# Linear attention and two MLPs on one core: one ring of five PSUM banks for attention, decoding exponents two pieces ahead, first loads released in turn

## The chip, the cores and the metric

The kernel runs on 1 core of one Trainium2 chip. The core has TensorE (PE, matmuls), VectorE (DVE), ScalarE (ACT), GpSimd (POOL), SyncE (SP, which here only issues transfers), an SBUF of 128 partitions and a PSUM of 8 banks of 512 floats per partition. The metric is device time in microseconds; before the change it is 1017.65 us, the median of 3 runs (1014.94 to 1017.94).

## The reference

Three stages follow each other; all in float32:

```python
# attention, batch 4, 8 heads, 576 tokens, head_dim 64, 128 features
proj = x @ omega.T;  h = proj - |x|^2/2;  h = h - max(h);  phi = exp(h) / sqrt(128)   # for q and for k
kv  = sum_s phi_k[s] v[s];  z = sum_s phi_k[s]
att = (phi_q @ kv) / (phi_q @ z + 1e-6)
# MLP 1: 2304 tokens, 512 -> 2048 -> 512
h = x @ w_in;  g = max(h, 0) + alpha * min(h, 0);  x = g @ w_out
# MLP 2: 512 -> 1536 -> 512
x = ((x @ w_a) * (x @ w_b)) @ w_out
```

The weights come to the kernel as 64-bit words and are made into floats by the kernel itself, as below.

## The kernel before, in words

The order of the instructions on each engine is written out by hand; the framework adds the waits. Tiles come from pools with a number of buffers; a new tile waits until an old one of its pool has had its last reader, and a pool opened in the place of a closed one waits for the closed one.

**Attention** goes in steps `s` (line 649 on). A unit `u` is a batch and four heads (8 units), and each has 5 token tiles `t`. One step makes the projections of a k tile and, from step 6 (`Q_LAG`), of a q tile into a pair of PSUM banks (`a_proj`, L523), takes their maxima on DVE (`a_max`, L532), the exponentials on ACT (`a_exp`, L546, one instruction per head, first all of the first bank, then all of the second), then adds the k tile of the step before to the `kv` sum (L559, one bank; at the end of a unit ACT copies it, L565), takes numerator and denominator of an older q tile (`a_num`: bank `nd`, normalised on DVE, L597 to L600, into `xn`), transposes the last exponentials (`a_t`: bank `tp`, copied by ACT or DVE, L577/L579, to `phT`), and transposes an older result into `xT` (`a_x`, bank `xp`, L612 to L620). So from step 10 on a step takes five banks of the tag `ps`.

**The weights** are 68 pieces of 128x512 words. A piece `p` (class `Decoder`) is loaded as `raw` (512 KB, L115, SP). ACT makes the exponent `z` from its high words (L127) and in way 0 scales the low words (L132): that is `start(p)`. `piece(p)` is a generator that is advanced one turn at a time from the other work (`go`): shift of z (DVE, L145), a (L147), c (L150, in ways 1 and 2 also L153), then the high part `wh` on ACT (L158) and the low part `wl` by two or three operations on POOL, or on DVE in way 2 (L157, L159, L160). A fifth turn starts the exponent of piece p+1, if `ahead` is set. `raw` has 2 buffers. `z` has one PSUM bank (`psz`) in steps 0 to 13, and two SBUF buffers after. The pieces go into `NS` slots of SBUF, of which 20 exist during attention; a piece whose slot still holds a weight in use waits (`can`). A credit (`step`) sets how many pieces a step may begin: none in steps 0 to 2, half a piece in steps 3 to 5, then one per step; in the later MLP stages 0.35 to 0.5 per 384 columns. The way of a piece is picked by planned loads of DVE, ACT and POOL.

**Stage 1** is steps 0 to 13 (`SPLIT_AT` = 14): attention and decoding of pieces 0 to 8 alone. The banks are: kv 1, `psz` 1, `ps` 6. The transfers of k, v, q and raw are issued in `attn_1`, before the maxima, with those of units 0 and 1 and raw 0 and 1 at once. **Stage 2** opens `ps` anew with 5 banks, and `psy` with 2 banks for MLP 1's output sums: five chunks of 256 tokens of MLP 1's first half run (`Mlp.run`), and within each front (`a_front`: 12 matmuls into a bank of `ps`, L265) one more attention step is interleaved (`attn_next`); its order is projections, MLP's `high` (ACT), maxima, `low` (DVE), exponentials, rest. The inputs of the MLP are split into a high and a low part (`split`: `xh` on ACT L251, `xl` on DVE or POOL L254). **Then** attention's memory is given back, the remaining slots are opened, and the rest of MLP 1 and MLP 2 run in chunks of 512 and 256 tokens, with fronts (L265) and backs (L331, L386) alternating on PE.

Of the kernel before, what the change touches and what calls it, by code (L numbers as in the profile page):

```python
# [9 lines left out]
F32 = mybir.dt.float32  # L10
F32R = mybir.dt.float32r
U32 = mybir.dt.uint32
# [3 lines left out]
PSUM = bass.MemoryType.PSUM  # L16
# [23 lines left out]
CHUNKS = (512, 512, 256, 512, 512)  # L40
NS = 29
NS1 = 20
# [10 lines left out]
def tile_kernel(ctx: ExitStack, tc: tile.TileContext, qT, kT, v1, omT, wbits, alpha, out):  # L53
# [44 lines left out]
    class Decoder:  # L98
# [12 lines left out]

        def load(self, p):
            if p < NP and p not in self.raw:
                raw = dec.tile([P, DM, 2], U32, tag="raw", name=f"raw{p}")
                nc.sync.dma_start(out=raw.rearrange("p n t -> p (n t)"), in_=wbits[p].bitcast(U32))  # L115
                self.raw[p] = raw

        def start(self, p):
# [6 lines left out]
            pool = self.bank or dec  # L125
            z = pool.tile([P, DM], U32, tag="z", name=f"z{p}", bufs=1 if self.bank else 2)
            nc.scalar.activation(z.bitcast(F32), H.bitcast(F32), AF.Copy, scale=2.0 ** -112)  # L127
# [7 lines left out]
        def piece(self, p):  # L135
            self.start(p)
            self.load(p + 1)
            z, way = self.z[p]
            raw = self.raw[p]
# [21 lines left out]
            self.ready = p + 1  # L161
            yield
            if self.ahead and self.can(p + 1):
                self.start(p + 1)

# [317 lines left out]

    t_k, t_q, t_v = {}, {}, {}
    phik, phiq, phT, kvt, xns = {}, {}, {}, {}, {}
    psp = [None]

    def load_k(u):
        t = ld.tile([P, 2 * S], F32, tag="k", name=f"k{u}")
        if u == 0:  # L490
            nc.scalar.dma_start(out=t[:, 0:256], in_=kT[u][:, 0:256])
            nc.sync.dma_start(out=t[:, 256:], in_=kT[u][:, 256:])
        else:
            nc.sync.dma_start(out=t, in_=kT[u])
        t_k[u] = t

    def load_v(u):
        t = ld.tile([P, TT * VC], F32, tag="v", name=f"v{u}")
        nc.sync.dma_start(out=t, in_=v1[u])
        t_v[u] = t  # L500

    def load_q(u):
        t = ld.tile([P, 2 * S], F32, tag="q", name=f"q{u}")
        nc.sync.dma_start(out=t, in_=qT[u])
        t_q[u] = t
# [132 lines left out]
    def attn_1(s):  # L638
# [3 lines left out]
        else:  # L642
            pair = None
        if s in ev["k"]:
            u, t = ev["k"][s]
            if t == 0 and u + 1 < U:
                load_k(u + 1)
            if t == 2 and u + 1 < U:
                load_v(u + 1)
            if u == 0 and t > 2:  # L650
                load_q(t - 3)
        if s in ev["q"]:
            u, t = ev["q"][s]
            if t == 4 and u + 2 < U:
                load_q(u + 2)
        return pair and (pair, jobs)

    def attn_2(s):

        D_.go(2)  # L660
        if s in ev["kv"]:
# [4 lines left out]
        if s in ev["t"]:  # L666
            a_t(*ev["t"][s])
        D_.go(2)

# [14 lines left out]

    st_p = ExitStack()
    st_m = ExitStack()
    A = Mlp(st_m, CI, 2)
    st_z = ExitStack()
    D_.bank = rpool(st_z, name="psz", bufs=1, space=PSUM)
    with ExitStack() as st:  # L690
        psp[0] = rpool(st, name="ps0", bufs=6, space=PSUM)
        w_ = bank("warm")
        for i in range(WARM):
            nc.tensor.matmul(w_[:, 0:P], lhsT=warm, rhs=warm, start=True, stop=True)
        for s in range(SPLIT_AT):
            D_.step(DEC0[0] if s < 3 else DEC0[1] if s < Q_LAG else DEC0[2])
            passed(1.3 if s < Q_LAG else 4.5)
            D_.ahead = s < SPLIT_AT - 1
            pj = attn_1(s)
            if pj:  # L700
                a_exp(*pj, a_max(*pj))
            if s == Q_LAG:
                nc.sync.dma_start(out=nalpha, in_=alpha)
# [12 lines left out]
    with st_m:  # L716
        psp[0] = rpool(st_p, name="ps1", bufs=5, space=PSUM)
        A.banks((psp[0], "ps"))
# [3 lines left out]
        def attn_next(high=None, low=None):  # L722
# [6 lines left out]
            if pj:  # L729
                nm = a_max(*pj)  # L730
            if low:
                low()
# [37 lines left out]
        while nxt_s[0] < steps:  # L770
            attn_more()
        st_p.close()
    st_a.close()
# [78 lines left out]
```

## Time and profile before

| | |
|---|---|
| median of 3 runs | 1017.65 us (1014.94 to 1017.94) |
| profiled execution | 1018.62 us, span 1016.8 us, mean granted clock 0.985 |
| PE busy | 983.3 us (97% of the span), 6414 matmuls |
| DVE, ACT, POOL busy | 481.8, 440.5, 270.1 us |
| PE on the chain that ended last | ab L265 29%, o L386 14%, h L265 14%, y L331 14% of the span |

A time in the trace counts from the start of the span; the execution's own time is 1.8 us longer. Busy time says how long an engine had an instruction running. A wait is idle time of an engine put down to what ended it. PEclk is the share of the full clock that TensorE was granted.

### The profile page before, as it was taken

The page shows a single profiled execution, that of the slowest core. Times are in us where ns is not written, and L with a number is a line of the kernel's source. Part 1 is how long each engine was busy: PE and PEld are TensorE (multiplying, and loading weights), DVE is VectorE, ACT ScalarE, POOL GpSimd, SP SyncE. Part 2 cuts the span into 40 slices and gives each one's busy share as a digit, 9 for nine tenths or more (in the row PEclk, how much of TensorE's full clock was granted, in tenths as well). Part 3 has the DMA queues.
Part 4 walks back from the last instruction along what each step waited for, and adds up shares of the span by engine and source line. Part 5 has one row for each costly group of instructions (what it writes and reads, how often), then busy time and mean ns, then how long its engine had stood idle before and what let it go on. Part 6 is the DMA issues. An engine that isn't in the chain of part 4 may idle for free.

```text
span 1016.8 us, 15843 instructions
## 1 busy us (share of the span) xinstructions
PE 983.3 (97%) x6414; PEld 840.3 (83%) x6414; DVE 481.8 (47%) x934; ACT 440.5 (43%) x1027; POOL 270.1 (27%) x208
## 2 busy tenths in 40 slices
PE   7869899999999999999999999999999999999998
PEld 6658799999988888889888888898888888898886
DVE  4868855654456666445465434344133322132132
ACT  5878766654455555445445332232232321122110
POOL 2856510000024543434233332332223220000100
PEclk7879999999999999999999999999999999999999
DMA  7543523000012332312212112121020302011021
GB/s 268 193 152 111 163 86 96 25 23 2 32 52 87 100 119 90 104 42 63 83 45 80 42 42 83 42 84 62 21 83 22 124 1 83 1 63 63 1 83 41
DMA packets 27449, 75.16 MB, mean 74 GB/s; under 512 B 2288, under 2 KB 5616, under 8 KB 27376
## 3 DMA queue, kind: packets, MB, share of 16 engines
q1 hardware_dynamic: 27232, 74.02, 22.1%
q8 instruction: 50, 0.82, 0.3%
q14 instruction: 23, 0.19, 0.1%
q10 hardware_dynamic: 144, 0.13, 0.0%
HBM read 59.99 MB, written 14.16 MB: 73 GB/s over the span
## 4 chain that ended last, share of the span: by engine, by line
PE 71%; DVE 0%; POOL 0%; issue 0%; ACT 0%; POOLq 0%; ACTq 0%
PE ab L265 29%; PE o L386 14%; PE h L265 14%; PE y L331 14%; DVE opl L396 0%; POOL xl L254 0%; POOL wl L160 0%; DVE xl L254 0%; DVE a L147 0%; ACT wh L158 0%; DVE h L291 0%; POOL a L159 0%; ACT gh L302 0%; ACT u L289 0%; ACT h L290 0%
## 5 line engine op out<-in xcount | busy, mean ns | idle before, releaser
L159 POOL TENSOR_TENSOR a<-a,wh 128x512 f32<-128x512 f32 x68 | 100.9, 1483 | 315.6 <-ACT wh L158 310.9
L265 PE MATMUL ab<-xh,wh 128*128 128x512 f32 (+1 forms) x480 | 177.3, 369 | 0.0
L265 PE MATMUL ab<-xh,wl 128*128 128x512 f32 (+1 forms) x480 | 177.2, 369 | 0.0
L265 PE MATMUL ab<-xl,wh 128*128 128x512 f32 (+1 forms) x480 | 177.1, 369 | 0.0
L265 PE MATMUL h<-xh,wh 128*128 128x512 f32 (+1 forms) x384 | 133.5, 348 | 1.0 <-ACT xh L251 1.0
L265 PE MATMUL h<-xl,wh 128*128 128x512 f32 (+1 forms) x384 | 130.5, 340 | 1.4 <-POOL xl L254 1.2
L331 PE MATMUL y<-gh,wh 128*128 128x512 f32 (+1 forms) x384 | 131.3, 342 | 0.0
L265 PE MATMUL h<-xh,wl 128*128 128x512 f32 (+1 forms) x384 | 130.3, 339 | 0.0
L331 PE MATMUL y<-gh,wl 128*128 128x512 f32 (+1 forms) x384 | 129.4, 337 | 0.0
L331 PE MATMUL y<-gl,wh 128*128 128x512 f32 (+1 forms) x384 | 129.3, 337 | 0.0
L291 DVE SCALAR_TENSOR_TENSOR h<-u,nalpha,h 128x256 f32<-128x256 f32 (+1 forms) x96 | 59.6, 621 | 119.5 <-ACT h L290 116.5
L254 POOL TENSOR_TENSOR xl<-xT,xh 128x512 fp32r<-128x512 f32 (+1 forms) x33 | 38.3, 1162 | 272.0 <-ACT xh L251 267.8
L371 DVE TENSOR_TENSOR ab<-a,ab 128x512 f32<-128x512 f32 (+1 forms) x60 | 38.4, 641 | 143.4 <-PE ab L265 140.5
L265 PEld LDWEIGHTS ab<-xl,wh 128*128 128x128 f32 x480 | 90.4, 188 | 16.2
L265 PEld LDWEIGHTS ab<-xh,wh 128*128 128x128 f32 x480 | 90.4, 188 | 16.0
L265 PEld LDWEIGHTS ab<-xh,wl 128*128 128x128 f32 x480 | 90.4, 188 | 15.8
L160 POOL TENSOR_TENSOR wl<-a,c 128x512 fp32r<-128x512 f32 x68 | 89.8, 1321 | 5.3
L272 ACT ACTIVATE gh<-ab 128x512 fp32r<-128x512 f32 (+1 forms) x60 | 33.4, 556 | 123.0 <-DVE ab L371 123.0
L386 PE MATMUL o<-wh,gh 128*128 128x512 f32 x216 | 84.5, 391 | 0.0
L386 PE MATMUL o<-wh,gl 128*128 128x512 f32 x216 | 84.5, 391 | 0.0
L386 PE MATMUL o<-wl,gh 128*128 128x512 f32 x216 | 84.4, 391 | 0.0
L265 PEld LDWEIGHTS h<-xl,wh 128*128 128x128 f32 x384 | 73.6, 192 | 10.2 <-POOL xl L254 1.6
(314 smaller groups left out, 1658.7 us busy)
## 6 DMA issues: line engine op xcount, KB each, us to landing
raw<-in_w SPq DMA_DIRECT2D x68, 512.0 KB, 3.7
v<-in_v SPq DMA_DIRECT2D x8, 650.0 KB, 5.4
q<-in_qT SPq DMA_DIRECT2D x8, 576.0 KB, 3.8
out<-opl SPq DMA_DIRECT2D x18, 256.0 KB, 2.1
yp<-ypart SPq DMA_DIRECT2D x4, 1024.0 KB, 7.1
opart<-op SPq DMA_DIRECT2D x4, 1024.0 KB, 5.0
opl<-opart SPq DMA_DIRECT2D x4, 1024.0 KB, 5.6
k<-in_kT SPq DMA_DIRECT2D x7, 576.0 KB, 4.7
```

Of the source, the lines that this page charges most:

```text
L159: eng.tensor_tensor(out=a, in0=a, in1=hi.bitcast(F32), op=ALU.subtract)
L160: eng.tensor_tensor(out=lo, in0=a, in1=c, op=ALU.add)
L254: (nc.vector, nc.gpsimd)[way].tensor_tensor(out=lo, in0=src, in1=hi.bitcast(F32), op=ALU.subtract)
L265: nc.tensor.matmul(hp, lhsT=w_[:, ks], rhs=r_, start=(i == 0), stop=(i == 3 * KT - 1))
L272: nc.scalar.activation(gh, g, AF.Copy)
L291: nc.vector.scalar_tensor_tensor(out=hp, in0=u_, scalar=nalpha[:, f:f + 1], in1=hp, op0=ALU.mult, op1=ALU.add)
L331: nc.tensor.matmul(ys[e], lhsT=w_[:, es], rhs=r_, start=(first and i == 0 and head), stop=(last and i == 2 and tail))
L371: nc.vector.tensor_tensor(out=pp[1], in0=a_, in1=pp[1], op=ALU.mult)
L386: nc.tensor.matmul(os_[t], lhsT=w_[:, ts_], rhs=r_, start=(i6 == 0 and i == 0), stop=(i6 == 5 and i == 2))
```

## The change

- Attention has one pool `ps` of five banks for both stages, opened once. `psz` has two banks and lies where `psy` is opened later.
- A piece has four turns instead of five; at the end of the fourth it starts the exponent of piece p+2, not p+1, and loads raw(p+2) as well when it begins. `raw` has 3 buffers, `NS` is 28 instead of 29. The exponents of pieces 0 and 1 are started in steps 3 and 4. In steps 11 to 13 no exponent is started ahead (before: in step 13 alone). Starting ahead no longer asks whether the slot is free.
- In attention, three turns are taken before kv and numerator and one before the transposes; before it was two, one and two after the transposes.
- The transfers are issued in a function of their own, `loads`, after the maxima. In steps 0 to 3 those of k1, raw0 and q0, v1, raw1 and q1 each wait for a one-column memset on DVE into the tile, which stands behind the step's maxima. The load of alpha moves from step 6 to step 7.

```diff
--- before.py
+++ after.py
@@ -38,7 +38,7 @@
 CB = 512
 REST = (512, 512)
 CHUNKS = (512, 512, 256, 512, 512)
-NS = 29
+NS = 28
 NS1 = 20
 
 DEC0 = (0.0, 0.5, 1.0)
@@ -109,9 +109,11 @@
             self.z = {}
             self.ahead = True
 
-        def load(self, p):
+        def load(self, p, after=False):
             if p < NP and p not in self.raw:
-                raw = dec.tile([P, DM, 2], U32, tag="raw", name=f"raw{p}")
+                raw = dec.tile([P, DM, 2], U32, tag="raw", name=f"raw{p}", bufs=3)
+                if after:
+                    after_dve(raw[:, :, 0].bitcast(F32))
                 nc.sync.dma_start(out=raw.rearrange("p n t -> p (n t)"), in_=wbits[p].bitcast(U32))
                 self.raw[p] = raw
 
@@ -123,7 +125,7 @@
             raw = self.raw[p]
             L, H = raw[:, :, 0], raw[:, :, 1]
             pool = self.bank or dec
-            z = pool.tile([P, DM], U32, tag="z", name=f"z{p}", bufs=1 if self.bank else 2)
+            z = pool.tile([P, DM], U32, tag="z", name=f"z{p}", bufs=2)
             nc.scalar.activation(z.bitcast(F32), H.bitcast(F32), AF.Copy, scale=2.0 ** -112)
             way = pick({"dve": 1.9, "act": 2.0, "pool": 3.9}, {"dve": 2.6, "act": 1.35, "pool": 2.6},
                        {"dve": 3.9, "act": 1.35})
@@ -135,6 +137,7 @@
         def piece(self, p):
             self.start(p)
             self.load(p + 1)
+            self.load(p + 2)
             z, way = self.z[p]
             raw = self.raw[p]
             L, H = raw[:, :, 0], raw[:, :, 1]
@@ -159,9 +162,8 @@
             eng.tensor_tensor(out=a, in0=a, in1=hi.bitcast(F32), op=ALU.subtract)
             eng.tensor_tensor(out=lo, in0=a, in1=c, op=ALU.add)
             self.ready = p + 1
-            yield
-            if self.ahead and self.can(p + 1):
-                self.start(p + 1)
+            if self.ahead:
+                self.start(p + 2)
 
         def can(self, p):
             return p < NP and p % NS < len(slots) and (p < NS or self.free.get(p - NS, False))
@@ -482,6 +484,11 @@
     kvp = [ac.tile([P, 4, D + 1], F32, name=f"kvp{i}") for i in range(3)]
 
     t_k, t_q, t_v = {}, {}, {}
+
+    def after_dve(t):
+
+        nc.vector.memset(t[:, 0:1], 0.0)
+
     phik, phiq, phT, kvt, xns = {}, {}, {}, {}, {}
     psp = [None]
 
@@ -491,16 +498,22 @@
             nc.scalar.dma_start(out=t[:, 0:256], in_=kT[u][:, 0:256])
             nc.sync.dma_start(out=t[:, 256:], in_=kT[u][:, 256:])
         else:
+            if u == 1:
+                after_dve(t)
             nc.sync.dma_start(out=t, in_=kT[u])
         t_k[u] = t
 
     def load_v(u):
         t = ld.tile([P, TT * VC], F32, tag="v", name=f"v{u}")
+        if u == 1:
+            after_dve(t)
         nc.sync.dma_start(out=t, in_=v1[u])
         t_v[u] = t
 
     def load_q(u):
         t = ld.tile([P, 2 * S], F32, tag="q", name=f"q{u}")
+        if u < 2:
+            after_dve(t)
         nc.sync.dma_start(out=t, in_=qT[u])
         t_q[u] = t
 
@@ -641,23 +654,35 @@
             pair, jobs = a_proj(ev["k"].get(s), ev["q"].get(s))
         else:
             pair = None
-        if s in ev["k"]:
+        return pair and (pair, jobs)
+
+    def loads(s):
+        if s < TT:
+
+            if s == 0:
+                load_k(1)
+            elif s == 1:
+                D_.load(0, True)
+                load_q(0)
+            elif s == 2:
+                load_v(1)
+            elif s == 3:
+                D_.load(1, True)
+                load_q(1)
+        elif s in ev["k"]:
             u, t = ev["k"][s]
             if t == 0 and u + 1 < U:
                 load_k(u + 1)
             if t == 2 and u + 1 < U:
                 load_v(u + 1)
-            if u == 0 and t > 2:
-                load_q(t - 3)
         if s in ev["q"]:
             u, t = ev["q"][s]
             if t == 4 and u + 2 < U:
                 load_q(u + 2)
-        return pair and (pair, jobs)
 
     def attn_2(s):
 
-        D_.go(2)
+        D_.go(3)
         if s in ev["kv"]:
             a_kv(*ev["kv"][s])
         if s in ev["num"]:
@@ -665,7 +690,6 @@
         D_.go()
         if s in ev["t"]:
             a_t(*ev["t"][s])
-        D_.go(2)
 
     def attn_3(s):
         if s in ev["x"]:
@@ -682,24 +706,26 @@
     nc.vector.tensor_scalar(out=om, in0=om_raw, scalar1=scale, scalar2=None, op0=ALU.mult)
     load_v(0)
 
-    st_p = ExitStack()
     st_m = ExitStack()
     A = Mlp(st_m, CI, 2)
     st_z = ExitStack()
-    D_.bank = rpool(st_z, name="psz", bufs=1, space=PSUM)
-    with ExitStack() as st:
-        psp[0] = rpool(st, name="ps0", bufs=6, space=PSUM)
+    psp[0] = rpool(st_a, name="ps", bufs=5, space=PSUM)
+    D_.bank = st_z.enter_context(tc.tile_pool(name="psz", bufs=2, space=PSUM))
+    if True:
         w_ = bank("warm")
         for i in range(WARM):
             nc.tensor.matmul(w_[:, 0:P], lhsT=warm, rhs=warm, start=True, stop=True)
         for s in range(SPLIT_AT):
             D_.step(DEC0[0] if s < 3 else DEC0[1] if s < Q_LAG else DEC0[2])
             passed(1.3 if s < Q_LAG else 4.5)
-            D_.ahead = s < SPLIT_AT - 1
+            D_.ahead = s < SPLIT_AT - 3
             pj = attn_1(s)
-            if pj:
-                a_exp(*pj, a_max(*pj))
-            if s == Q_LAG:
+            nm = a_max(*pj)
+            loads(s)
+            a_exp(*pj, nm)
+            if s in (3, 4):
+                D_.start(s - 3)
+            if s == Q_LAG + 1:
                 nc.sync.dma_start(out=nalpha, in_=alpha)
             attn_2(s)
             attn_3(s)
@@ -714,7 +740,6 @@
     D_.ahead = True
 
     with st_m:
-        psp[0] = rpool(st_p, name="ps1", bufs=5, space=PSUM)
         A.banks((psp[0], "ps"))
         nxt_s = [SPLIT_AT]
         due = [0.0]
@@ -728,6 +753,7 @@
                 high()
             if pj:
                 nm = a_max(*pj)
+            loads(s)
             if low:
                 low()
             if pj:
@@ -769,7 +795,6 @@
         A.run([(0, CI * i, CI, range(NF0), False) for i in range(NCI)], beside, ready)
         while nxt_s[0] < steps:
             attn_more()
-        st_p.close()
     st_a.close()
 
     w2 = ctx.enter_context(tc.tile_pool(name="w2", bufs=1, side=RIGHT))
```

## Rows read from the trace of the kernel before

**Rows 1.** Page, part 1: busy us, share of the span, instructions of each engine.
```profile
PE 983.3 (97%) x6414; PEld 840.3 (83%) x6414; DVE 481.8 (47%) x934; ACT 440.5 (43%) x1027; POOL 270.1 (27%) x208
```

**Rows 2.** Waits of PE, 0 to 62: us in total, times, longest.
```profile
PE pp(2, 4)_False L523 <- ACT xh L251: 7.0, 1, 7.0
PE kv L559 <- ACT kvp L565: 3.2, 1, 3.2
PE kv L559 <- DMA v<-in_v: 3.2, 1, 3.2
PE nd L593 <- DVE phT L577: 2.5, 1, 2.5
```

**Rows 3.** Windows: length, busy us of five engines, PEclk, DMA share, GB/s.
```profile
19.60:47.10 27.50, 21.72 (x290) 18.22 (x290) 25.34 (x50) 24.44 (x72) 21.23 (x17) 0.81 0.59 195
47.10:60.50 13.40, 5.89 (x80) 5.08 (x82) 9.30 (x23) 8.22 (x25) 8.34 (x8) 0.82 0.38 113
400.00:1016.80 616.80, 611.90 (x2900) 511.00 (x2898) 233.63 (x382) 191.23 (x359) 139.87 (x104) 1.00 0.17 56
```

**Rows 4.** DMA, 0 to 20 in 40 slices, raw's landing there, in all.
```profile
GB/s 0 0 0 39 190 386 382 416 351 333 343 347 385 384 359 356 389 380 390 397 430 409 425 412 446 409 389 429 344 115 66 114 126 276 341 315 98 0 0 0
raw<-in_w SPq DMA_DIRECT2D x3, 512.0 KB, 10.7
...
raw<-in_w SPq DMA_DIRECT2D x68, 512.0 KB, 3.7
```

**Rows 5.** Timeline of the start: start, us, instruction, idle time before it.
```profile
5.09 0.76 DVE L532 TENSOR_REDUCE nm(0, 0, 0)_182<-pp(0, 0)_False 128x2 f32<-128x256 f32 x2 [1.46 <-PE pp(0, 0)_False L523]
20.63 0.40 ACT L565 ACTIVATE kvp<-kv 128x260 f32<-128x260 f32 x1
20.89 0.91 ACT L546 ACTIVATE ph<-pp(1, 1)_False,nm(0, 1, 1)_333 128x128 f32<-128x128 f32 x3
```

**Rows 6.** Timeline around the pool change: ACT, DVE, POOL, PE.
```profile
51.03 0.63 ACT L127 ACTIVATE z<-raw 128x512 f32<-128x512 f32 x1 [1.23 <-DMA raw<-in_w]
51.60 0.65 ACT L132 ACTIVATE raw<-raw 128x512 f32<-128x512 uint32 x1
54.37 2.18 ACT L546 ACTIVATE ph<-pp(2, 3)_False,nm(0, 2, 3)_764 128x128 f32<-128x128 f32 x8 [1.52 <-DVE nm(0, 2, 3)_764 L532]
52.58 1.15 DVE L254 TENSOR_TENSOR xl<-xT,xh 128x256 fp32r<-128x256 f32 x2 [3.15 <-ACT xh L251]
53.66 1.28 DVE L532 TENSOR_REDUCE nm(0, 2, 3)_764<-pp(2, 3)_False 128x4 f32<-128x512 f32 x2
54.86 0.68 DVE L145 TENSOR_SCALAR z<-z 128x512 uint32<-128x512 uint32 x1
56.24 0.15 DVE L597 TENSOR_SCALAR rc<-nd 128x4 f32<-128x4 f32 x1
56.98 0.42 DVE L150 TENSOR_SCALAR c<-a 128x512 uint32<-128x512 uint32 x1
57.53 1.29 POOL L157 TENSOR_TENSOR c<-raw,c 128x512 f32<-128x512 f32 x1 [4.41 <-ACT xT L620]
61.61 0.73 POOL L254 TENSOR_TENSOR xl<-xT,xh 128x256 fp32r<-128x256 f32 x1
62.40 0.36 PE L265 MATMUL h<-xh,wh 128*128 128x256 f32 x1
```

**Rows 7.** DVE's timeline at step 14; a wait of PE, 62 to 140.
```profile
62.77 0.43 DVE L145 TENSOR_SCALAR z<-z 128x512 uint32<-128x512 uint32 x1 [1.82 <-ACT z L127]
PE pp(4, 1)_False L523 <- DVE xn L600: 0.7, 1, 0.7
```

**Rows 8.** PE's timeline, projection of step 12.
```profile
43.87 0.60 PE L523 MATMUL pp(2, 2)_False<-om,k 64*128 64x128 f32 x5 [0.55 <-ACT ph L546]
```

**Rows 9.** Last piece on POOL; PE on the chain that ended last.
```profile
819.13 1.29 POOL L160 TENSOR_TENSOR wl<-a,c 128x512 fp32r<-128x512 f32 x1
835.84 5.59 PE ab L265 x24
```

## The prediction

> **What bounds the kernel now.** I read the page's busy times first: TensorE (PE) is busy 983.3 of 1016.8 us, the next engine 481.8 [rows 1]. Then the windows: from 400 us to the end PE is busy 611.9 of 616.8 us at granted clock 1.00 [rows 3], so nothing can be gained there except by PE work, which the change leaves alone. All that is open lies ahead of the first MLP matmul at 62.40 us. PE's waits in the first 62 us name four places: 3.2 us for the first v transfer, 3.2 us for ScalarE's (ACT) copy of the first kv sum, 2.5 us for a phT copy, and 7.0 us at step 14, where the six-bank pool is closed and the five-bank pool opened [rows 2]. Those 15.9 us are the prize. But a wait of PE is worth only what the engines that feed it can use. So I looked next at VectorE (DVE): in 19.6 to 47.1 us it is busy 25.34 of 27.5 us, and in 47.1 to 60.5 us (the two steps around the pool change) 9.30 of 13.4 [rows 3]. In the first stretch at most 2.2 us can be saved without taking work off DVE, in the second at most 4.1. This pair of numbers decides my forecast more than PE's waits do.
>
> **Part 1, the start (transfers let go in turn, first exponents early).** Now all loads leave SP at once; the raw transfers of the first 20 us take 10.7 us to land against 3.7 in the whole run [rows 4], since they queue behind k, v and q at 380 to 430 GB/s. After: om, k0 and v0 (1.36 MB by the tile shapes) are alone, and at the row's rate, from 2.0 us, done near 5.9, landed near 6.5; the first kv can start when its exponentials are there, about 6.8, so that some 2 of its 3.2 us of wait go. k1 waits for a memset behind the first maximum, which ends at 5.85 [rows 5], so its bytes come at about 7.4, and the transfers stand still for 1.5 us. Each later one is freed by the maximum of its step and finds others still moving. Behind k1 come raw0, q0, v1, raw1, q1, raw2, 4.0 MB with k1, 10.3 us at 390 GB/s: raw1 lands near 15.3 and raw2 near 18.1. Six memsets of one column cost DVE about 0.15 us each (a 128x4 row of DVE takes 0.15 [rows 6]) at a time when it is idle.
> What follows on ACT, which runs in order: z(0) after the exponentials of step 3, z(1) after those of step 4 (held by raw1 to 15.3), wh(0), z(2) (held by raw2 to 18.1), and only then the exponentials of step 5 (half of the 2.18 us of a full step [rows 6]), the kvp copy at about 20.0 and the exponentials of step 6 at 20.4. Before, kvp ran at 20.63 and step 6 at 20.89 [rows 5]. So of the two 3.2 us waits almost nothing is left: the earlier start is spent in front of two raw transfers. I take -0.4 us. Bounds: -4.4 if the raws do not hold ACT (step 6's q could be there at 12.4, its v at 14), +3 if each release comes a step later than I have it.
> A rule of the Trainium skill speaks against this part: DMA: Bandwidth & Descriptors, section Rules for kernel authors, says to issue a transfer early and wait for it late, so that its fixed setup cost overlaps. The row above (10.7 against 3.7 us) shows that early issue here hides nothing for those that are issued last. By the rule the 1.5 us standstill is pure loss, and this term would be about 1.5 us better without it; by the row v0 gains 2 us from it.
>
> **Part 2, steps 7 to 12 (five banks, z two pieces ahead, four turns a piece).** The third raw buffer looks like slack, but raw(p+2) is now loaded where raw(p+1) was, waits for the same reader of raw(p-1), and z(p+2) stands where z(p+1) stood. So ACT is held by the raw transfer as before. DVE no longer needs z just in time, but with 92% busy it was not waiting for it. The decoder's share of DVE, ACT and POOL (GpSimd) instructions is unchanged, except which of three ways a piece takes. The phT copy of a step now stands behind wh and z on ACT; it has a step of slack. Five banks with five tiles a step make the next projection wait for all exponentials of the step, where six let it begin after half of them (it waited 0.55 us for that half in step 12 [rows 8]). Bounds: -2.2 (DVE's idle time) to +4.4 (below). I take 0.
>
> **Part 3, steps 12 to 14.** Now ACT waits 1.23 us for raw(8), makes z(8) (0.63) and scales raw (0.65), and only then the two xh splits; DVE waits 3.15 us for them and starts step 13's maximum at 53.66 [rows 6]. After, no exponent is started at the end of steps 11 and 12, so 2.5 us drop out: with step 12's exponentials, wh, phT and xh in a row I get that maximum at 51.5. But z(8) is now made inside piece 8, behind step 13's exponentials: 51.5 + 0.65 + 2.18 + 0.65 with hand-offs is 55.1. DVE's shift for piece 8 stood at 54.86. DVE's stall has moved from before the maximum to after it. From there the order is three decode instructions, then the normalisation, so c(8) ends at 57.0 instead of 57.40, and POOL, whose c, a, wl and xl chain from 57.53 ends at 62.34 and feeds the first MLP sum at 62.40 [rows 6], is 0.4 us earlier. PE's projection of step 14 itself, the 7.0 us wait, comes near 54.5; PE then waits for phT and POOL instead. I take -0.4. Bounds: -4.1 (DVE's idle time in the window) to +1.
>
> **Part 4, steps 14 to 16.** Pieces 9 and 10 both lack a started z: the ends of pieces 7 and 8 start none, and piece 9 starts 11. For piece 9 this was so before (DVE waited 1.82 us [rows 7]). For piece 10 it is new: z(10) stands behind step 15's exponentials, DVE meets its shift some 2 us later, xn(15) follows, and the second bank of step 16's projection needs that bank. By hand the delay is up to 1.4 us; the nearest row, a projection that waits for xn, is 0.7 [rows 7]. I take +0.7, bounds 0 to 2.3. From here PE has no slack, so this counts fully.
>
> **Part 5, the rest.** NS 28 instead of 29: pieces 44 and 60 wait for a slot where 45 and 61 did, so the last pieces come one piece later, 12.5 us by the code's rate (two pieces in three steps of a 5.6 us front [rows 9] and a back of half that). wl of piece 67 is ready at 820.4, and the back that needs it starts at 841.4 [rows 9]: 21 us of cover, cost 0; without the cover, at most a piece's 3 us. Exponents 20 and 21 are made about 160 us before use, ACT time in a stretch where PE is the bound. The shared two banks go from z to y long after z(8). PE's later waits keep their causes. I take 0, bounds -3 to +3.
>
> **Sum.** -0.4 + 0 - 0.4 + 0.7 + 0 = -0.1 us. The profiled execution took 1018.62 (span 1016.8, 1.8 around it), 0.97 above the median of 1017.65, so 1018.5 on its scale, **1017.5** for a median.
>
> **Rivals.**
> *The stall closes (1011).* z(8) and z(10) do not hold DVE, because the exponentials in front of them come earlier or DVE has other work; the idle time of DVE at the pool change goes (-4.1) and ACT is held less at the start (-2.4): -6.5. For it: PE's 7.0 us is real and its bank rule is gone. Against: the order on ACT above.
> *All four PE waits go (1002).* 1017.65 - 15.9. For it: PE is the bound afterwards. Against: DVE's 92%.
> *The fifth bank costs (1022, the slower side).* Place: projections of steps 9 to 14. Price: the second half of 2.18 us of exponentials, 1.09 us a step, less the 0.36 us that DVE idles per step now, 0.73 by six steps, +4.4 with the sum above. It decides once exponentials, projection, first maximum and hand-offs (2.18 + 1.2 + 0.65 + 0.4 = 4.4) exceed the present step, which is 4.4 too. For it: that equality. Against: most projections are made while DVE is still at decode.
> That the change does not do what it says, a stall that only moves, is my forecast itself.
>
> **Chances.** Forecast 0.44 (0.10 of it faster by over 0.3%, 0.28 within, 0.06 slower), stall closes 0.26 (0.24 faster), all waits 0.10 (faster), fifth bank 0.20 (0.16 slower, 0.04 within). Faster 0.44, within 0.3% (3.1 us, about what a measurement here can tell) 0.34, slower 0.22. Range 1007 to 1023: outside lie the all-waits case and the tails of two others, 0.2 in all. The forecast alone: 1014 to 1021.
>
> **What would show it.** Part 1: step 6's exponentials near 20.4 and ACT waiting for raw before z(1) and z(2); if they come before 18, the stall rival gains. Part 3: step 13's maximum near 51.5, then DVE waiting about 2 us for z(8), first MLP sum at 61.5 to 62. Part 4: a DVE wait for z(10) and a PE wait for xn at step 16. Part 5: no PE wait after 400 us. I am wrong if the first MLP sum starts before 59 or after 65 us, or if PE's waits after it change by over 3 us.

## The result and the profile after

The change makes the kernel slower: 1025.91 us median of 4 runs (1024.82 to 1028.74) against 1017.64 us before, a ratio of 1.0091 (95% interval 1.0064 to 1.0119). The forecast of 1017.5 us, and its range up to 1023, were too low. The profiled execution after took 1028.74 us (span 1026.8), 2.8 above its median, so differences read from it are a little too large.

Part 1 of the page and the clock row of part 2 after, for [rows 1]:

```profile
PE 992.5 (97%) x6414; PEld 848.7 (83%) x6414; DVE 478.3 (47%) x937; ACT 441.2 (43%) x1027; POOL 272.4 (27%) x211
...
PEclk8769989999999999999999999999999999999999
```

PE runs the same 6414 matmuls but is busy 9.2 us longer. More busy time for the same work points to a lower granted clock rather than to waits (the mean granted clock is 0.975 after, 0.985 before). To place it, I cut both spans at the same matmuls (projection of step 7, of step 13, the first MLP sum `h`, projection of step 17, of step 26, the last `o`; starts from PE's timeline, us). The last column is the best version found below.

| stretch | before | after | difference | e9_best |
|---|---|---|---|---|
| start to step 7 | 21.89 | 23.23 | +1.3 | 20.33 |
| step 7 to 13 | 25.41 | 28.73 | +3.3 | 25.40 |
| step 13 to first `h` | 15.10 | 11.02 | -4.1 | 14.13 |
| first `h` to step 17 | 14.22 | 19.65 | +5.4 | 14.20 |
| step 17 to 26 | 59.28 | 59.97 | +0.7 | 57.66 |
| step 26 to the last `o` | 876.82 | 880.13 | +3.3 | 876.88 |

Kernels with the same program in attention differ here too: before, e6, e7 and e11 by up to 2.0 us in one of the first five rows, after and e10 by up to 1.8. The +0.7 is not clear of that; of the +3.3 of steps 7 to 13, 1.5 is (e10 takes 26.89). The stretch from the first `h` to step 17 is clear: it takes 18.5 to 19.7 us in the four kernels with after's break in the exponents (after, e3, e8, e10) and 13.5 to 16.6 in the twelve others. With the stretch ahead of it, where the four are early, it is 30.3 to 31.3 against 26.9 to 30.2. Behind the first `h` PE is idle 2.5 us longer and busy 6.9 us longer, after and then before:

```profile
62.98:1026.80 963.82, 947.12 (x5868) 810.26 (x5868) 435.94 (x843) 399.61 (x906) 241.92 (x182) 0.99 0.20 64
```

```profile
62.40:1016.80 954.40, 940.20 (x5870) 803.40 (x5868) 439.95 (x844) 397.90 (x903) 237.13 (x177) 1.00 0.20 65
```

PE's waits of the first 62 us after, for [rows 2] (us in total, times, longest):

```profile
PE kv L572 <- ACT kvp L578: 6.3, 1, 6.3
PE nd L606 <- ACT phT L592: 3.9, 2, 2.3
PE kv L572 <- ACT ph L559: 3.1, 3, 1.7
```

The 7.0 us wait at the pool change and the v wait are gone. In their place the wait for the kvp copy has grown from 3.2 to 6.3 us, and phT, now copied late by ACT, holds PE 3.9. Of the 3.1 us by which the kvp wait has grown, 1.1 is the copy itself (21.71 against 20.63) and 2.0 is PE, which gets there earlier (step 6's projection starts at 14.71 against 16.70). ACT's timeline of the start, for [rows 5], shows why the copy is late (start, length, instruction, idle time before it):

```profile
13.52 0.64 ACT L559 ACTIVATE ph<-pp(0, 4)_False,nm(0, 0, 4)_279 128x128 f32<-128x128 f32 x2
17.43 0.62 ACT L129 ACTIVATE z<-raw 128x512 f32<-128x512 f32 x1 [3.27 <-DMA raw<-in_w]
17.99 0.61 ACT L161 ACTIVATE wh<-a 128x512 fp32r<-128x512 f32 x1
20.14 0.63 ACT L129 ACTIVATE z<-raw 128x512 f32<-128x512 f32 x1 [1.54 <-DMA raw<-in_w]
20.71 1.12 ACT L559 ACTIVATE ph<-pp(1, 0)_False,nm(0, 1, 0)_314 128x128 f32<-128x128 f32 x4
21.71 0.40 ACT L578 ACTIVATE kvp<-kv 128x260 f32<-128x260 f32 x1
```

ACT has nothing to do from 14.1 to 17.4 us but cannot go on: z(1) and z(2) stand in its order ahead of step 5's exponentials and the kvp copy, and their raw has not landed. SP's queue in the same stretch:

```profile
12.23 0.33 SPq L117 DMA_DIRECT2D raw<-in_w  x1
12.65 0.38 SPq L517 DMA_DIRECT2D q<-in_qT  x1
13.08 0.43 SPq L117 DMA_DIRECT2D raw<-in_w  x1
```

Raw 1 leaves only when step 3's maximum has passed, and raw 2, which nothing holds, stands in SP's order behind the held q1. Its z can start at 20.14. The holding also leaves a gap in the transfers. From 5.5 to 8.0 us the queues move 105 GB/s (the last number), where e9_best, with nothing held, moves 343; after and then e9_best:

```profile
5.50:8.00 2.50, 0.76 (x16) 0.60 (x14) 1.45 (x7) 1.95 (x8) 0.00 (x0) 1.00 0.45 105
```

```profile
5.50:8.00 2.50, 1.09 (x14) 0.83 (x12) 1.51 (x4) 1.95 (x8) 0.00 (x0) 1.00 0.97 343
```

That is 0.6 MB less. At the 370 GB/s that the changed kernel moves from 8 to 17 us it is 1.6 us, an estimate from these rows.

DVE's timeline at the pool change after, and ACT at step 16, for [rows 6, 7]:

```profile
54.15 1.28 DVE L545 TENSOR_REDUCE nm(0, 2, 3)_768<-pp(2, 3)_False 128x4 f32<-128x512 f32 x2
57.60 0.70 DVE L148 TENSOR_SCALAR z<-z 128x512 uint32<-128x512 uint32 x1 [2.17 <-ACT z L129]
64.31 0.43 DVE L148 TENSOR_SCALAR z<-z 128x512 uint32<-128x512 uint32 x1 [1.83 <-ACT z L129]
71.73 0.43 DVE L148 TENSOR_SCALAR z<-z 128x512 uint32<-128x512 uint32 x1 [1.48 <-ACT z L129]
...
75.86 0.66 ACT L129 ACTIVATE z<-raw 128x512 f32<-128x512 f32 x1 [2.25 <-DMA raw<-in_w]
76.42 0.58 ACT L592 ACTIVATE phT<-tp 128x512 f32<-128x512 f32 x1
```

Pieces 8, 9 and 10 all find no exponent made and wait for it inside the step; then z(12) waits for raw with step 16's phT behind it. Last, windows of three stretches (columns as in [rows 3], the eighth number is PEclk), after and then before:

```profile
19.60:47.10 27.50, 19.46 (x244) 16.23 (x244) 20.33 (x39) 23.73 (x71) 17.42 (x14) 0.75 0.55 187
60.00:73.50 13.50, 11.71 (x81) 10.33 (x82) 8.76 (x24) 10.26 (x29) 6.89 (x6) 0.51 0.49 160
476.00:492.00 16.00, 14.00 (x85) 12.67 (x84) 6.75 (x12) 7.04 (x16) 7.39 (x6) 0.89 0.12 33
```

```profile
60.00:73.50 13.50, 11.38 (x136) 10.28 (x136) 8.32 (x23) 10.31 (x29) 8.09 (x8) 0.79 0.51 171
476.00:492.00 16.00, 14.80 (x70) 11.99 (x70) 8.98 (x15) 7.20 (x14) 6.64 (x6) 1.00 0.16 46
```

From 60 to 73.5 us PE is equally busy before and after (11.4, 11.7), but after, the clock is 0.51: almost the whole stretch at the lower of the two levels (1.2 of 2.4 GHz). There a matmul of `h` starts 0.21 us behind the one before it; at the upper level it is 0.12.

### The profile page after: what moved, and what is told of

Same layout as the page of the kernel before. It is cut to its first block, busy times and chain, and to the rows that moved or that the text cites. A ratio compares the mean times of both kernels' runs of the same rounds, so it can differ in the third digit from the quotient of the medians.

```text
span 1026.8 us, 15877 instructions
## 1 busy us (share of the span) xinstructions
PE 992.5 (97%) x6414; PEld 848.7 (83%) x6414; DVE 478.3 (47%) x937; ACT 441.2 (43%) x1027; POOL 272.4 (27%) x211
## 4 chain that ended last, share of the span: by engine, by line
PE 70%; DMA 1%; DVE 1%; POOL 0%; ACT 0%; issue 0%; SPq 0%; POOLq 0%; ACTq 0%
PE ab L267 28%; PE o L388 14%; PE h L267 14%; PE y L333 14%; DMA raw<-in_w 1%; DVE opl L398 0%; POOL a L162 0%; POOL wl L163 0%; POOL xl L256 0%; DVE op L401 0%; DVE xl L256 0%; DVE a L150 0%; ACT z L129 0%; ACT xh L253 0%; DVE h L293 0%
## 5 line engine op out<-in xcount | busy, mean ns | idle before, releaser
L256 POOL TENSOR_TENSOR xl<-xT,xh 128x512 fp32r<-128x512 f32 (+1 forms) x36 | 41.6, 1159 | 261.1 <-ACT xh L253 261.1
L267 PEld LDWEIGHTS h<-xl,wh 128*128 128x128 f32 x384 | 74.7, 194 | 10.9 <-POOL xl L256 2.4
```

The costliest lines, as they stand in the source:

```text
L256: (nc.vector, nc.gpsimd)[way].tensor_tensor(out=lo, in0=src, in1=hi.bitcast(F32), op=ALU.subtract)
L267: nc.tensor.matmul(hp, lhsT=w_[:, ks], rhs=r_, start=(i == 0), stop=(i == 3 * KT - 1))
```

## The experiments

Every time is a median of 4 to 10 runs; the ratio is to runs of the kernel before that were taken beside them (4 for the changed kernel, 19 to 29 for the others), and 0.001 is 1.0 us. A profile is of one execution: that of after is the slowest of its four, that of e12 the fastest of its nine (1016.78). In the edits the switches of the kernels are replaced by their values, and e8's is written as its effect. The theory: the loss is the place of the exponents `z` on ACT, ahead of attention's work and of raw that hasn't landed. Rivals: the fifth bank; the held transfers by themselves; fewer slots.

| kernel | us | ratio (95%) |
|---|---|---|
| after | 1025.91 | 1.0091 (1.0064 to 1.0119) |
| e1_ring_alone | 1017.16 | 0.9999 (0.9987 to 1.0010) |
| e2_no_exp | 1016.70 | 0.9998 (0.9982 to 1.0014) |
| e3_no_loads | 1021.32 | 1.0040 (1.0026 to 1.0055) |
| e4_keep | 1022.07 | 1.0043 (1.0025 to 1.0060) |
| e5_keep_late_one | 1021.28 | 1.0033 (1.0022 to 1.0044) |
| e6_ns28 | 1017.85 | 1.0001 (0.9991 to 1.0010) |
| e7_late_two | 1020.19 | 1.0023 (1.0011 to 1.0035) |
| e8_no_hold | 1023.06 | 1.0052 (1.0036 to 1.0068) |
| e9_best | 1015.23 | 0.9976 (0.9966 to 0.9985) |
| e10_after_late_old | 1022.40 | 1.0047 (1.0027 to 1.0067) |
| e11_late_four | 1019.17 | 1.0015 (1.0004 to 1.0026) |
| e12_keep_late_old | 1020.34 | 1.0025 (1.0015 to 1.0035) |
| e13_held_late_exp | 1019.65 | 1.0014 (1.0000 to 1.0027) |
| e14_held_raw_first | 1016.44 | 0.9988 (0.9973 to 1.0003) |

### The three parts alone: e1, e2, e3, e8

e1_ring_alone is the kernel before with the one pool:

```diff
-    D_.bank = rpool(st_z, name="psz", bufs=1, space=PSUM)
-        psp[0] = rpool(st, name="ps0", bufs=6, space=PSUM)
+    psp[0] = rpool(st_a, name="ps", bufs=5, space=PSUM)
+    D_.bank = st_z.enter_context(tc.tile_pool(name="psz", bufs=1, space=PSUM))
...
-        psp[0] = rpool(st_p, name="ps1", bufs=5, space=PSUM)
```

> The kernel before with one part alone: one pool of five banks opened once, psz still one bank, exponents one piece ahead, loads as before. Theory (exponents' place on ACT and their raw transfers make the change slow): the ring by itself is harmless, 1013 to 1018 us, PE's 7.0 us wait at step 14 gone or shrunk below 4 us. Rival 'fifth bank': this alone gives most of the loss, 1022 us or more, with PE waits for exponentials in front of projections of steps 9 to 14. Rival 'held loads': 1013 to 1018.

e2_no_exp adds the function `loads` with its memsets to e1 and leaves the decoder as before. e3_no_loads is the changed kernel with the transfers issued behind `attn_1`, ahead of the maxima, as before (`loads_old`), without memsets:

```diff
             pj = attn_1(s)
+            loads_old(s)
             nm = a_max(*pj)
-            loads(s)
```

> The changed kernel with the decoder of the kernel before: exponents one piece ahead, two raw buffers, 29 slots, five turns; ring and held loads stay. Theory: the loss is gone, 1012 to 1018 us; step 6's exponentials before 20 us. Rival 'held loads': still 1021 or more. Rival 'fifth bank': still 1021 or more.

> The changed kernel with the loads of the kernel before (all first transfers issued at once, loads ahead of the maxima); ring and exponents two ahead stay. Theory: the loss stays but for the start: ACT's waits for raw before z(1) and z(2) (3.27 and 1.54 us in the changed kernel) shrink, 1021 to 1025 us. Rival 'held loads': 1018 or less. Rival 'fifth bank': no change, 1024 to 1027.

e8_no_hold is the changed kernel, its order of transfers kept, without the memsets:

```diff
     def after_dve(t):
-
-        nc.vector.memset(t[:, 0:1], 0.0)
+        pass
```

> The changed kernel without the six memsets: the first transfers go in the new order but are not held. If the holding makes the exponents 1 and 2 late on ACT, raw 1 and 2 land earlier, the wait of PE for kvp falls from 6.3 us towards e3_no_loads (pp(2,4) near 52 to 53), and the time is near 1021 to 1022 us. If the new order or the place after the maxima does it, 1026 us and the 6.3 us wait stay.

The ring is free, with an interval of a tenth of a per cent to either side, and so it is together with the held transfers (e2, where step 6's exponentials, expected before 20 us, came at 20.65). The fifth bank falls as a cause, and the held transfers by themselves too. In e1 PE's wait at the pool change shrinks from 7.0 to 3.4 us, and the time stays as it was. The new decoder costs without the held transfers (e3, +4.0 by ratio); the 3.8 us that e7 and e11 below lose behind attention are as large as that, so that an early exponent in attention need not cost anything where nothing is held. But the parts do not add: 0, 0 and 4 stand against 9. Taking the memsets alone out of the changed kernel (e8) gives back 4.0 by ratio. Its 1023.06 us lies between the 1021 to 1022 expected if the holding is to blame and the 1026 of the new order. PE's kvp wait is still 6.1 us long, and ACT still waits 3.23 and 1.39 us for raw 1 and raw 2, which I had not expected, but all of it ends earlier: z(2) starts at 18.87 instead of 20.14, step 7's projection at 21.96 instead of 23.23. Whether the new order costs beside the old one (e8 against e3, 1.2 us) is within the intervals and open.

### The broken chain: e4

Steps 11 to 13 start exponents too, and those from piece 9 on go to SBUF:

```diff
-            D_.ahead = s < SPLIT_AT - 3
+            D_.ahead = True
...
-            pool = self.bank or dec
+            pool = (self.bank if p < 9 else None) or dec
```

> The changed kernel with the exponents started two pieces ahead without the break at steps 11 to 13 (z of piece 9 and later in the two SBUF buffers): z(8), z(9) and z(10) are there before DVE needs them. Theory: DVE's waits of 2.17, 1.83 and 1.48 us for them go, the first MLP sum starts near 60.5 instead of 63 us, and step 17's projection near 78 instead of 82.6; 1019 to 1022 us. Rivals 'held loads' and 'fifth bank': the waits go but something else takes their place, 1024 to 1027.

4.9 us of the loss go (1.0091 to 1.0043; with the late decoder of before, e10 to e12, it is 2.2). 1022.07 us is at the upper end of what was expected. In e4 step 17's projection came at 77.63, as expected, but the first `h` at 63.72, not near 60.5. DVE's four shifts at steps 13 to 16 in e12, which has the same edit, answer to the first lines shown of after; none waits:

```profile
56.51 0.68 DVE L154 TENSOR_SCALAR z<-z 128x512 uint32<-128x512 uint32 x1
62.32 0.43 DVE L154 TENSOR_SCALAR z<-z 128x512 uint32<-128x512 uint32 x1
68.18 0.42 DVE L154 TENSOR_SCALAR z<-z 128x512 uint32<-128x512 uint32 x1
74.96 0.42 DVE L154 TENSOR_SCALAR z<-z 128x512 uint32<-128x512 uint32 x1
```

and the clock from 60 to 73.5 us is 0.86 there, in e10 with the chain broken 0.58:

```profile
60.00:73.50 13.50, 12.48 (x154) 10.81 (x154) 9.42 (x26) 9.80 (x28) 10.56 (x9) 0.86 0.57 188
```

```profile
60.00:73.50 13.50, 11.78 (x88) 10.27 (x88) 8.76 (x25) 10.24 (x29) 6.83 (x7) 0.58 0.47 163
```

In the profiles of all four kernels with the chain broken the clock of this stretch is 0.51 to 0.72, in those of the twelve others 0.79 to 1.00.

### After attention: e6, e7, e11, e5, e10, e12

e6_ns28 is the kernel before with `NS = 28`. e7_late_two is the kernel before with NS 28, three raw buffers, and two pieces ahead after attention (`lag` is 2 there and 1 earlier); e11_late_four is the kernel before with four turns a piece there. e5 is e4 with `lag` 1 after attention; e10 and e12 are the changed kernel and e4 with `lag` 1 and five turns after attention. The edit, with its values for e10 and e12:

```diff
-            self.load(p + 2)
+            if self.lag == 2:
+                self.load(p + 2)
...
+            if self.turns == 5:
+                yield
-            if self.ahead:
-                self.start(p + 2)
+            if self.ahead and (self.lag == 2 or self.can(p + 1)):
+                self.start(p + self.lag)
...
         X.banks()
         D_.credit = 0.0
+        D_.lag, D_.turns = 1, 5
```

> The kernel before with NS 28 in place of 29 and nothing else. Late depth: as before, 1017.5 us, within 1. Fewer slots: 1020 to 1022, with waits of ACT for raw and of PE for the MLP's copies at the pieces 44 and 60.

> The kernel before with NS 28, three raw buffers and, from the part after attention on, exponents two pieces ahead; attention as before. Late depth: 1020 to 1022, with the two late waits of PE. Fewer slots: the same 1020 to 1022, but then e6_ns28 has it too. Neither (the late loss needs the changed start): 1017.5.

> The kernel before with four turns a piece instead of five after attention, nothing else. If the turns make the late wait of PE for ACT's copy a (1.3 us in e5_keep_late_one): 1019 to 1020, with that wait. If they don't: 1017.5 to 1018.

> The changed kernel with its exponent chain not broken at step 11 (as in e4_keep) and, from the part after attention on, exponents one piece ahead and only if the slot is free, with NS 28 and three raw buffers kept. Late depth (the exponents two ahead stand on ACT before their raw has landed and hold the MLP's copies behind them): the late waits of 2.0 and 1.0 us go and the settled gain of 1.6 us stays to the end, 1016 us. Fewer slots (NS 28 alone makes pieces 44 and 60 late): no change against e4_keep, 1022. Early start (something that the first 140 us leave behind): 1022 too.

> The changed kernel with the decoder of before after attention (one ahead, five turns; NS 28 and three raw buffers kept). If the late part is worth what e7_late_two lost (2 to 2.4 us) and the four turns as much as the late wait for ACT's copy (1 to 1.3 us): 1022 to 1023. If only attention counts: 1025 to 1026.

> e4_keep (held loads, chain not broken) with the decoder of before after attention. If the rest of the loss of e5_keep_late_one (3.3 us) is the four turns of the late part: 1017 to 1018.5. If it is in attention (the held loads with early exponents, the granted clock there): 1020 to 1021.

The slot costs nothing (e6). Two ahead costs 2.3 us (e7, with the 28 slots of e6 and a third raw buffer) and four turns 1.5 (e11, with nothing else changed), each in the kernel before; going back to before in both gives the changed kernel 4.5 us (e10) and e4 1.8 (e12). e5, with the depth alone, gained only 1.0, within its interval of nothing: a miss, since the turns were still in it. e10 and e11 came where they were expected, and e12 where it was expected if the rest of the loss is in attention. PE's waits after 400 us show two places, in after, in e7 and in e11:

```profile
PE h L267 <- POOL xl L256: 2.0, 1, 2.0
PE ab L267 <- ACT a L372: 1.2, 1, 1.2
```

```profile
PE h L274 <- POOL xl L263: 2.0, 1, 2.0
```

```profile
PE h L275 <- POOL xl L264: 1.2, 1, 1.2
PE ab L275 <- ACT a L380: 1.0, 1, 1.0
```

The first wait is 1.2 us before as well. POOL's timeline there, after and then before:

```profile
479.68 1.31 POOL L160 TENSOR_TENSOR c<-raw,c 128x512 f32<-128x512 f32 x1 [9.63 <-DVE c L153]
480.95 1.82 POOL L162 TENSOR_TENSOR a<-a,wh 128x512 f32<-128x512 f32 x1
482.85 1.60 POOL L163 TENSOR_TENSOR wl<-a,c 128x512 fp32r<-128x512 f32 x1
484.42 1.26 POOL L256 TENSOR_TENSOR xl<-xT,xh 128x512 fp32r<-128x512 f32 x1
```

```profile
473.32 1.60 POOL L159 TENSOR_TENSOR a<-a,wh 128x512 f32<-128x512 f32 x1 [9.08 <-ACT wh L158]
475.00 1.62 POOL L160 TENSOR_TENSOR wl<-a,c 128x512 fp32r<-128x512 f32 x1
476.58 1.71 POOL L254 TENSOR_TENSOR xl<-xT,xh 128x512 fp32r<-128x512 f32 x1
```

The way of a piece is picked when its exponent is started. Started a piece earlier, under other planned loads, this piece (41) takes way 0, with one operation more on POOL ahead of the MLP's `xl`. The second wait is ACT's, after:

```profile
684.33 0.66 ACT L129 ACTIVATE z<-raw 128x512 f32<-128x512 f32 x1 [4.14 <-DMA raw<-in_w]
684.89 0.37 ACT L372 ACTIVATE a<-ab 128x256 f32<-128x256 f32 x1
```

An exponent waits 4.14 us for its raw, and behind it stands the copy that PE needs. This one comes with the four turns alone (e11: z waits 3.96 us for raw at 672.45), which bring the exponent forward from the fifth turn to the end of the fourth.

### Holding the transfers under early exponents: e9, e13, e14

e9_best is e12 with the transfers as before (the edit of e3). e13 is e12 without early exponents:

```diff
-            D_.ahead = True
+            D_.ahead = s >= 7
...
-            if s in (3, 4):
-                D_.start(s - 3)
...
             if self.ahead and (self.lag == 2 or self.can(p + 1)):
+                self.start(p + 1)
                 self.start(p + self.lag)
```

e14 is e12 with the first two raws let go at once:

```diff
             if s == 0:
+                D_.load(0)
+                D_.load(1)
                 load_k(1)
             elif s == 1:
-                D_.load(0, True)
                 load_q(0)
...
-                D_.load(1, True)
                 load_q(1)
```

> Ring of five banks, first transfers as before, exponents two ahead in attention with the chain not broken at step 11, and after attention the decoder as before (one ahead, five turns; NS 28). If the changed kernel's loss lies in the held loads, the broken chain and the late part, each of which is taken out here, the early gain of e3_no_loads at pp(2,4) (6.2 us) stays in part: 1013 to 1016 us. If the exponents two ahead in attention are themselves what costs (ACT's queue, the four turns): 1019 to 1021.

> e12_keep_late_old (first transfers held, chain kept, late decoder of before) without early exponents: none started in steps 3 and 4, and two ahead only from step 7 on. If the held loads cost only because z(1) and z(2) then stand on ACT before raw 1 and raw 2 have landed, the copy kvp comes near 19.5 instead of 21.5 us, PE's wait for it falls from 7.6 us to 4 to 5, and the time is that of e9_best, 1015 to 1016.5. If holding the transfers costs by itself (k, v or q late): 1020.

> e12_keep_late_old with raw 0 and raw 1 issued at once in step 0, unheld, ahead of k1; k1, q0, v1 and q1 still held, early exponents kept. If raw on ACT is the cause: no wait of z for raw, kvp near 19.5, and 1015 to 1017. If the cause is the held k, v or q: 1020. In between if raw 2, which is issued by piece 0, is what comes late: its z stands ahead of the exponentials of step 5 either way.

e9 is the only kernel faster than before (interval 0.9966 to 0.9985) and 5.0 us faster than e12, which differs from it only in the transfers; in the two profiles step 7's projection starts at 20.33 and at 23.01. ACT's timelines of e12, e9 and e14:

```profile
17.23 0.62 ACT L134 ACTIVATE z<-raw 128x512 f32<-128x512 f32 x1 [4.59 <-DMA raw<-in_w]
19.93 0.63 ACT L134 ACTIVATE z<-raw 128x512 f32<-128x512 f32 x1 [1.53 <-DMA raw<-in_w]
21.50 0.40 ACT L586 ACTIVATE kvp<-kv 128x260 f32<-128x260 f32 x1
```

```profile
16.15 0.66 ACT L134 ACTIVATE z<-raw 128x512 f32<-128x512 f32 x1 [0.98 <-DMA raw<-in_w]
17.69 0.63 ACT L134 ACTIVATE z<-raw 128x512 f32<-128x512 f32 x1 [0.34 <-DMA raw<-in_w]
19.26 0.40 ACT L586 ACTIVATE kvp<-kv 128x260 f32<-128x260 f32 x1
```

```profile
14.13 0.68 ACT L134 ACTIVATE z<-raw 128x512 f32<-128x512 f32 x1
18.52 0.62 ACT L134 ACTIVATE z<-raw 128x512 f32<-128x512 f32 x1 [2.66 <-DMA raw<-in_w]
20.07 0.40 ACT L586 ACTIVATE kvp<-kv 128x260 f32<-128x260 f32 x1
```

With raw 0 and 1 free and k, v, q still held (e14), 3.8 of the 5.0 us come back, and what is left of ACT's wait is for raw 2, which SP issued at 12.72, behind the held q1, where e9 had issued all three raws by 6.6. Early issue alone does not bring raw sooner: in e12 raw 2 left SP at 11.40, 1.7 us earlier than in after, and its z started only 0.2 us earlier (19.93 against 20.14). The gap in the transfers is in e12 as in after (128 GB/s from 5.5 to 8.0 us) and not in e14 (369), so e14 mends two things at once and does not tell them apart. Together with e2, which has the gap too (125) and loses nothing, the holding is dear only with early exponents: it makes raw late, and ACT's order hands that on. e13 was to show it from the other side and does not. The kvp copy came early as expected (18.80), but the exponents of pieces 1 and 2 then stood inside their steps, and PE lost it there to waits of kv for exponentials, 6.2 us in five of them. Its 1019.65 is near the 1020 expected if the holding costs by itself; since its trace shows another loss, it separates nothing, and against that reading stands e2.

## Why the prediction was wrong, step by step

The steps that failed most are Part 4, which priced one wait and no change of the granted clock, and Part 5, which put two edits behind attention at nothing.

- **Part 1** (-0.4) had the order on ACT right, and both waits for raw, but not their size. I put kvp at 20.0 and step 6's exponentials at 20.4; they came at 21.71 and 21.98. I had the 1.5 us standstill, but behind it I let the transfers follow each other at full rate, and I read 380 to 430 GB/s from a row that has 333 to 446. On the chip raw 1 left SP at 12.23 and raw 2, behind the held q1, at 13.08: raw 2 could be used at 20.1, not 18.1. The first row of the table is +1.3, within my bounds: the kernels with the attention of before have 21.06 to 22.19 in that row, after and e10 23.23 and 24.26. The 5.0 us by which held transfers cost under early exponents (e12 against e9) are not this term: I counted from the kernel before, and from there e12 is +2.5 in all. With nothing held, the chain kept and the late decoder of before, the early exponents come with a gain of 2.4 us (e9); the holding turns this around. I credited the held start with v's 2 us; that gain exists only as far as ACT's order lets it through.
- In that step I weighed a rule of the Trainium skill (DMA: Bandwidth & Descriptors, Rules for kernel authors: issue early, wait late) against a row, and went by the row. The rule had the sign: e9, with everything issued at once, beats e12, and the standstill is there (105 against 343 GB/s). e2 shows its limit, for holding cost nothing there.
- **Part 2** (0) became +3.3 in the profiled run, within its bounds but for none of the reasons given. Five banks cost nothing (e1). The argument of DVE's 92% holds as far as it went: even e9 takes 25.40 us for steps 7 to 13, against 25.41 before. But it only rules out a gain. After, DVE is busy just 20.33 of the same 27.5 us, so it was not DVE that held this stretch. PE's waits for phT and exponentials (3.9 and 3.1 us in the first 62) and the clock (0.75 against 0.81) are larger than before; what each of them cost there is not shown. By e10, which has the same program up to here, the runs bear out 1.5 of the 3.3.
- **Part 3** (-0.4) named the right stall: DVE waits 2.17 us for z(8), and the first `h` comes at 62.98, later than the 61.5 to 62 that I gave, but between the 59 and 65 beyond which I would have called myself wrong. The stretch gained 4.1 us, all of my bound, not 0.4. The maximum of step 13 came at 54.15, not 51.5, since the kernel was 4.7 us late by then. Step 14's projection did come early (56.06 against 58.14), for nothing.
- **Part 4** (+0.7, at most 2.3) is the term that the trace shows furthest off. From the first `h` to step 17 the loss is 5.4 us. I priced one wait for xn and put the granted clock at nothing, without a reason. The runs show that the pieces 8 to 10 all wait, and that PE then ran that stretch almost wholly at the lower clock. My sum counts waits alone, and behind the first `h` PE lost 2.5 us of idle time and 6.9 us of longer busy time. Keeping the chain takes back 2.2 to 4.9 us. Parts 3 and 4 together were +0.3 as predicted and +1.3 in the profile: what the pool change gains, the pieces behind it lose.
- **Part 5** (0) has NS right, and exactly: e6 is 1.0001. It missed the two other edits that reach past attention: the depth (+2.3, e7) and the four turns (+1.5, e11), through the picked way and through z ahead of the MLP's copies. Together that is 3.8, and +3.3 in the trace behind step 26, where my bounds were 3 to either side. I had said that a PE wait after 400 us would show me wrong; one such wait, 1.2 us, was there before, and after there are two, 3.2 in all.
- **The rivals.** The slower side did decide, but not by the mechanism that I gave it: the fifth bank is free. "The stall closes" is nearest to e9, where the chain and the start are mended, and it is worth 2.4 us there, not 6.5. What was lacking among the rivals is the mechanism of this result: exponents out of place on ACT, which runs in order, too early for their raw at four places (z(1), z(2), z(12), and at 684 us) and too late for DVE at three (pieces 8 to 10), and the clock behind them.

The parts of the loss don't add up to one sum: from e9 (-2.4) to after (+9.3), holding the transfers costs 5.0 us (e12), breaking the chain then 2.2 (e10), and the late decoder then 4.5; with the last two in the other order it is 1.8 for the decoder and 4.9 for the chain. The intervals of these steps are 1.4 to 3.5 us wide to either side, so the split is open. The sign of the first is beyond them; of the other two, whichever is taken last is clear of its interval, and the other is not. Not tried: the exponents' way fixed independently of when they start, and raw 2 issued early in the held order.

## What to carry to other kernels

Work that is moved ahead on an engine that runs in order must have its data there: check the landing of each transfer against its new place, or the early work becomes a wait for everything behind it. A busy engine next to the bound says that nothing can be gained there, not that nothing can be lost. And an edit in a helper that runs through the whole kernel has to be priced in every stage that calls it, planned choices included.

## What the runs showed of the hardware

Much of the difference between the two kernels can be in the granted clock. The share not granted, one minus a run's mean clock, times its span, is an estimate of the most that the lower level can have cost; it is 13.6 us on average over 29 runs of the kernel before (those beside e1 to e4) and 20.7 over the 4 of after. That is 7.1 of the 8.7 us between their means (1017.6 and 1026.3). It is not so for every step: e11, slower than before by its ratio of 1.0015, has 12.4.

Waits of PE of 0.4, 0.6 and 1.6 us (at 56.06, 57.09 and 60.28 in its timeline) stood ahead of the long stretch at 0.51. A single one of 2.0 us near 480 us stood ahead of a dip that takes the window 476 to 492 to 0.89, in after, in e7 and in e8, where before, with a wait of 1.2, it stayed at 1.00. But in e3 and e4 the same wait of 2.0 us was followed by no dip (1.00), so the length of a wait does not settle it. Where there was a dip, the price of a wait was the wait and some of the matmuls behind it at half rate. The Trainium skill (TensorE: Matmul & The Clock Gate, Part 1: The HAM clock gate) says that PE's clock is set by how busy it has been lately; the rows with a dip agree, and those of e3 and e4 neither show it nor speak against it.

Letting transfers go in turn made each one faster, but raw 1 and raw 2 were not there sooner: the raws of the first 14 us took 5.5 us each to land, against 10.9 before and 10.7 in e9, and z(1) and z(2) could start at 17.43 and 20.14, against 16.15 and 17.69 in e9.
